# Building the weights' float32 on one core in another way: two bitwise DVE steps with an operand in PSUM, no GpSimd multiplication

## The chip, the cores and the metric

The kernel runs on one core of one Trainium2 chip. The metric is the device time of one execution in microseconds (us); the time of a kernel is the median of several runs. PE is TensorE, DVE is VectorE, ACT is ScalarE, POOL is GpSimd, SP is the engine that issues the DMAs.

## The reference

```python
scores = q @ k.T / 8                                  # 4 batches, 8 heads, 576 rows, 64 per head
scores = where(scores >= max(scores) - tau, scores, -1e9)
x = softmax(scores) @ v                               # (4, 576, 512)
u = x + (relu(x.T @ w_tok1) @ w_tok2).T               # 576 -> 256 -> 576, over the rows
u = u + relu(u @ w_ch1) @ w_ch2                       # 512 -> 1536 -> 512
h = relu(u @ w_in)                                    # 512 -> 1024
out = (h * sigmoid(conv3(h, conv_w))) @ w_out         # 1024 -> 512
```

q, k, v are float32. The six weights arrive as float64, which no engine computes with: a value is two 32-bit words, 8 bytes apart from the next. Each weight is turned on the chip into two float16 matrices, a high part and a low part (the rest), and a product is made of three matmuls: high with high, high with low, low with high.

## The kernel before, in words

The four batches run one after the other, and each has two parts. `attention(b)` (L432) goes through 36 slots of 128 query rows (4 pairs of heads, 9 slots each). For a slot, `scores` (L279) makes matmuls into two PSUM banks, `exps` (L300) takes the maximum on DVE (L303) and the exponential on ACT (L315), `mask` (L319) multiplies with the mask on DVE (L322), `ph` (L324) makes the float16 high part on ACT (L327), `rest` (L329) the low part on POOL (L331) and a transposing DMA, and `pv` (L338) multiplies with v into bank 7. After a pair of heads, `tok` (L379) computes the token mixing, with one bank at a time from the list `free`.

`dense(b)` (L486) has four loops: L526 (u with w_ch1, 24 groups of 12 matmuls), L544 (with w_ch2, 8 groups of 36), L577 (with w_in, 16 groups of 12) and L601 (with w_out). Each group takes a bank from `free` (`dbank`, L271, the oldest first). The evacuation of a group is issued after the next group's matmuls (`flush`, L478), and then the bank goes back into `free`. Evacuations are ACT and then DVE for L526 (L500, L501), DVE for most of L544 (L508 and what follows), ACT for L577 (L553). While `dense(b)` runs, the steps of `attention(b + 1)` are issued between its groups.

Of the 8 PSUM banks, attention 0 uses 0 to 5 for scores in turn (L282), later batches 0 to 3; bank 7 takes `pv`; bank 6 is in `free` from the start. When attention 0 is through with its scores, L459 adds banks 4 and 5:

```python
free = [6]                                # L269
free.extend((4, 5))                       # L459
```

The weights are converted in 47 chunks of at most 512 columns: 3 of w_tok1, 4 of w_tok2 (288 columns each), 12 of w_ch1, 12 of w_ch2, 8 of w_in, 8 of w_out. `wload` (L142) is a generator: its first step issues the DMA into a staging tile `st` (3 buffers), its second all the arithmetic. `wstep` (L166) does one second step and one more first step. It is called eight times in attention 0 (`W0`, L616), once for each of the 12 rounds of L526, three times for each of the 4 rounds of L544, twice for each of the 8 rounds of L577, all in batch 0. A scheduler that works ahead of the run puts the instructions into the engines' queues by a simulated time, so that a chunk can stand earlier in a queue than in the program; each queue is worked off in order.

For a chunk `load_f32` (L107) does: ACT multiplies the high word, read as a float32, by 256 in place (L125); DVE shifts the high word by 3 and masks it (L126); DVE masks the high word and sets an exponent (L128); DVE adds the top three bits of the low word (L134, or for w_tok1 and w_tok2 a DVE shift, L131, and a POOL addition, L132); POOL multiplies the two (L137). Then ACT rounds to float16, the high part (L150), and POOL subtracts it from the float32, the low part (L151). The float32 lies in a tile `wf` with two buffers.

Of the kernel before, what the change touches and what calls it, by code (L numbers as in the profile page):

```python
# [8 lines left out]
F32 = mybir.dt.float32  # L9
F16 = mybir.dt.float16  # L10
I32 = mybir.dt.int32
AF = mybir.ActivationFunctionType
# [6 lines left out]
def kernel(ctx: ExitStack, tc: tile.TileContext, q, k, v, tau,  # L19
# [7 lines left out]
    nc = tc.nc  # L27
# [19 lines left out]
    WS = 2.0 ** UP  # L47
    SX = VSC / ONE
    UDS = 1.0 / (WS * WS)

# [56 lines left out]
    def load_f32(src, o, n, up=0, early=False):  # L107

        if src.dtype == F32:
            g = tmpp.tile([P, 512], F32, tag="wf", name="wf")
            nc.sync.dma_start(g[:, :n], src[:, o:o + n])
            return lambda: g[:, :n]
        st = stage.tile([P, 512, 2], I32, tag="st", name="st")
        with hold("w"):
            nc.sync.dma_start(st[:, :n].rearrange("p n w -> p (n w)"), src.bitcast(I32)[:, 2 * o:2 * (o + n)])

        def bits():
            lo, hi = st[:, :n, 0], st[:, :n, 1]
            f = tmpp.tile([P, 512], I32, tag="wf", name="wf")
            f, hf = f[:, :n], hi.bitcast(F32)
            A.activation(out=hf, in_=hf, func=AF.Copy, scale=256.0)  # L125
            V.tensor_scalar(out=f, in0=hi, scalar1=3, scalar2=0x3FFFFFF8,  # L126
                            op0=ALU.logical_shift_left, op1=ALU.bitwise_and)
            V.tensor_scalar(out=hi, in0=hi, scalar1=-0x40000000, scalar2=(63 + up) << 23,  # L128
                            op0=ALU.bitwise_and, op1=ALU.bitwise_or)
            if early:  # L130
                V.tensor_scalar(out=lo, in0=lo, scalar1=29, scalar2=None, op0=ALU.logical_shift_right)  # L131
                G.tensor_tensor(out=f, in0=f, in1=lo, op=ALU.add)  # L132
            else:
                V.scalar_tensor_tensor(out=f, in0=lo, scalar=29, in1=f,  # L134
                                       op0=ALU.logical_shift_right, op1=ALU.bitwise_or)
            f = f.bitcast(F32)
            G.tensor_tensor(out=f, in0=f, in1=hf, op=ALU.mult)  # L137
            return f

        return bits  # L140

    def wload(src, dst, o, n):  # L142
        wide = src.dtype != F32
        f = load_f32(src, o, n, UP if wide else 0, src in (w_tok1, w_tok2))
        yield
        f = f()
        hi, lo = [d[:, o:o + n] for d in dst]
        if not wide:
            G.tensor_scalar(out=f, in0=f, scalar1=WS, scalar2=1.0, op0=ALU.mult, op1=ALU.mult)
        A.activation(out=hi, in_=f, func=AF.Copy)  # L150
        G.tensor_tensor(out=lo, in0=f, in1=hi, op=ALU.subtract)  # L151
        yield
# [6 lines left out]
    for src, pr, step in ((w_tok1, wt1, 512), (w_tok2, wt2, 288), (w_ch1, wc1, 512),  # L159
                                (w_ch2, wc2, 512), (w_in, wi, 512), (w_out, wo, 512)):  # L160
        tot = src.shape[1]
        wq += [(src, flat(pr), o, min(step, tot - o)) for o in range(0, tot, step)]

    wrun = []

    def wstep(n):  # L166

        for _ in range(n):
            while wq and len(wrun) < 3:
                wrun.append(wload(*wq.pop(0)))  # L170
                next(wrun[-1])
            if wrun:
                next(wrun.pop(0))
            if wq:
                wrun.append(wload(*wq.pop(0)))
                next(wrun[-1])
# [255 lines left out]
    def attention(b):  # L432
# [18 lines left out]
        while i < c1 + LAG or todo:  # L451
# [3 lines left out]
            if c0 <= i - 1 < c1:  # L455
                mask(i - 1)
                ph(i - 1)
                if i == PER:
                    free.extend((4, 5))  # L459
# [232 lines left out]
```

## Time and profile before

| | us |
|---|---|
| median of 3 runs | 836.05 (835.38 to 837.16) |
| the profiled execution | 839.7 |
| its span, first to last instruction | 837.9 |
| busy in the span: PE, DVE, ACT, POOL | 735.2, 598.1, 478.0, 452.8 |

The busy share of an engine over the whole span is a mean over stages with different limits: attention 0 with nothing dense beside it, then four dense parts, the first with the conversion of the weights, the last with no attention beside it. So the views of single stretches say more than the sums. A busy instruction of DVE or POOL can contain waiting for the other.

### The profile page before, as it was taken

What the parts mean: (1) busy time and instruction counts of PE and PEld (TensorE: products, weight loads), DVE (VectorE), ACT (ScalarE), POOL (GpSimd) and SP (SyncE); (2) the same over time, 40 slices, a digit from 0 to 9 for tenths busy, and PEclk for the clock granted to TensorE, in tenths of its full rate; (3) what the DMA queues carried; (4) which work ended last, traced back from release to release, by engine and by line L of the source; (5) the groups of instructions that cost most, each with busy time, mean ns of one, the idle gap of its engine ahead of it and who ended that gap; (6) DMA issues with size and microseconds to landing.
All of it is one profiled execution on the core that took longest, in us unless ns stands there. A gap on an engine that the chain in (4) does not pass through costs nothing. (4 is left out here: it accounts for less than half of the span.)

```text
span 837.9 us, 18667 instructions
## 1 busy us (share of the span) xinstructions
PE 735.2 (88%) x7376; PEld 552.4 (66%) x7376; DVE 598.1 (71%) x954; ACT 478.0 (57%) x993; POOL 452.8 (54%) x444
## 2 busy tenths in 40 slices
PE   4767858788878667999999988999999999999988
PEld 2555646567656555577888765677888765787754
DVE  6898988999999999525777797257775881232370
ACT  6867866565566676534656676346655762220361
POOL 5878887788888889611545465124545640000041
PEclk8998999999999998999999999999999999999999
DMA  6999899888898762423767753326644411000001
GB/s 205 216 181 220 166 204 257 193 215 201 198 197 188 193 145 63 100 64 81 146 137 142 148 109 71 86 51 142 131 82 79 74 31 51 8 1 1 2 1 56
DMA packets 197543, 101.38 MB, mean 121 GB/s; under 512 B 174544, under 2 KB 178128, under 8 KB 197456
## 3 DMA queue, kind: packets, MB, share of 16 engines
q1 hardware_dynamic: 197456, 100.20, 54.8%
q8 instruction: 57, 0.93, 0.5%
q14 instruction: 30, 0.25, 0.1%
HBM read 42.36 MB, written 4.72 MB: 56 GB/s over the span
## 5 line engine op out<-in xcount | busy, mean ns | idle before, releaser
L331 POOL TENSOR_TENSOR ph<-e,ph 128x576 f16<-128x576 f32 x108 | 150.2, 1393 | 110.6 <-ACT ph L327 98.2
L544 PE MATMUL ps<-act_t,wc_h 128*128 128x256 f16 (+1 forms) x768 | 151.7, 288 | 0.0
L526 PE MATMUL ps<-u_h,wc_h 128*128 128x256 f16 (+1 forms) x384 | 110.5, 288 | 11.0 <-DVE act_t L501 10.9
L322 DVE SCALAR_TENSOR_TENSOR e<-ps,thr,e 128x576 f32<-128x576 f32 x108 | 87.2, 811 | 42.7 <-ACT e L315 22.1
L303 DVE TENSOR_REDUCE nm<-ps 128x1 f32<-128x576 f32 x144 | 107.3, 746 | 12.5 <-PE ps L291 10.7
L567 POOL TENSOR_TENSOR act_t<-ct,act_t 128x576 f16<-128x576 f32 x32 | 45.5, 1421 | 125.9 <-ACT act_t L566 122.9
L526 PE MATMUL ps<-u_l,wc_h 128*128 128x256 f16 (+1 forms) x384 | 110.5, 288 | 0.7 <-DVE u_l L411 0.7
L544 PE MATMUL ps<-act_t,wc_l 128*128 128x256 f16 (+1 forms) x384 | 110.5, 288 | 0.0
L526 PE MATMUL ps<-u_h,wc_l 128*128 128x256 f16 (+1 forms) x384 | 110.4, 288 | 0.0
L327 ACT ACTIVATE ph<-e 128x576 f16<-128x576 f32 x108 | 73.3, 680 | 58.1 <-DVE e L322 32.8
L291 PE MATMUL ps<-kt,qt 128*128 128x288 f16 (+1 forms) x480 | 76.2, 296 | 20.4 <-DVE e L322 20.3
L311 POOL TENSOR_SCALAR thr<-nm,mtaus 128x1 f32<-128x1 f32 x108 | 52.0, 482 | 73.0 <-DVE nm L303 67.9
L501 DVE SCALAR_TENSOR_TENSOR act_t<-ps,act_t 128x256 f16<-128x256 f32 (+1 forms) x96 | 43.2, 452 | 64.7 <-ACT act_t L500 64.6
L526 PEld LDWEIGHTS <-wc_h 128*128 128x128 f16 x768 | 75.0, 98 | 21.4 <-issue 2.3
L544 PEld LDWEIGHTS <-wc_h 128*128 128x128 f16 x768 | 75.4, 98 | 19.8 <-issue 0.9
L346 PE MATMUL ps<-vh,pt 128*128 128x65 f16 (+1 forms) x1080 | 73.3, 196 | 12.9 <-DVE x L366 8.0
L315 ACT ACTIVATE e<-ps,bias 128x576 f32<-128x576 f32 x108 | 79.7, 738 | 8.1 <-POOL ph L331 2.1
L577 PE MATMUL ps<-u_h,wi_h 128*128 128x256 f16 (+1 forms) x256 | 75.7, 296 | 9.8 <-ACT h L553 4.6
L562 DVE SCALAR_TENSOR_TENSOR ct<-h,cw,ct 128x576 f32<-128x576 f32 x64 | 77.1, 1205 | 9.5 <-ACT ct L560 8.7
L601 PE MATMUL ps<-wo_h,act_t 128*128 128x512 f16 x256 | 77.3, 381 | 1.2 <-POOL act_t L567 0.7
L577 PE MATMUL ps<-u_h,wi_l 128*128 128x256 f16 (+1 forms) x256 | 75.8, 296 | 0.0
L577 PE MATMUL ps<-u_l,wi_h 128*128 128x256 f16 (+1 forms) x256 | 75.7, 296 | 0.0
(111 smaller groups left out, 1720.8 us busy)
## 6 DMA issues: line engine op xcount, KB each, us to landing
st<-in_moe_w_ch_dram SPq DMA_DIRECT2D x24, 512.0 KB, 4.7
ld<-in_v_dram SPq DMA_DIRECT2D x32, 288.0 KB, 3.9
kt<-ks SPq DMA_DIRECT2D x48, 144.0 KB, 2.7
st<-in_moe_w_in_dram SPq DMA_DIRECT2D x8, 512.0 KB, 4.1
st<-in_moe_w_out_dram SPq DMA_DIRECT2D x8, 512.0 KB, 4.3
out_dram<-ot SPq DMA_DIRECT2D x16, 256.0 KB, 2.0
ld<-in_q_dram SPq DMA_DIRECT2D x12, 288.0 KB, 3.7
ld<-in_k_dram SPq DMA_DIRECT2D x12, 288.0 KB, 3.4
```

The source lines that it names most:

```text
L291: T.matmul(s3[o:o + m, a], st["qt"][:, hh, q0:q0 + m], st["kt"][hh][:, x, a * hn:(a + 1) * hn], start=(x == 0), stop=(x == 1))
L303: crit["max"] = V.tensor_reduce(out=nm, in_=c["s3"], axis=AX.XY, op=ALU.max, negate=True)
L315: crit["exp"] = A.activation(out=e.rearrange("p (a b) -> p a b", a=2), in_=c["s3"], func=AF.Exp, bias=bias, scale=sc)
L322: crit["mask"] = V.scalar_tensor_tensor(out=e3, in0=c["s3"], scalar=c["thr"], in1=e3, op0=ALU.is_ge, op1=ALU.mult)
L327: A.activation(out=c["ph"][:, 0:S], in_=c["e"], func=AF.Copy)
L331: G.tensor_tensor(out=c["ph"][:, S:], in0=c["e"], in1=c["ph"][:, 0:S], op=ALU.subtract)
L346: T.matmul(dst[o:o + m], pt[:, j, o:o + m], vh[:, hh, j, 0:D + 1], start=(j == 0), stop=(j == NSL - 1))
L526: T.matmul(t, wc1[wx][:, f, c], u[c][ux][:, sl], start=(c == 0 and i == 0), stop=(c == NC - 1 and i == 2))
L544: T.matmul(t, wc2[wx][:, c, f], r_t(f, rx)[:, sl], start=(by_dve(c) and f == 0 and i == 0), stop=(f == NF - 1 and i == 2))
L562: V.scalar_tensor_tensor(out=ct, in0=ht[:, kk:kk + S], scalar=cw[:, kk, f:f + 1], in1=ct, op0=ALU.mult, op1=ALU.add)
L577: T.matmul(t, wi[wx][:, f, c], u[c][ux][:, s0:s0 + n], start=(c == 0 and i == 0), stop=(c == NC - 1 and i == 2))
L601: T.matmul(t, g_t(f, gx)[:, j * P:(j + 1) * P], wo[wx][:, f], **lim)
```

## The change

`wload` now starts a chunk in `load_hl`, which gives two views of the staging tile: the upper 16 bits of the low word as unsigned 16-bit integers, and the high word. `float32` then issues four instructions. ACT multiplies the high word, read as a float32, by a power of two in place. ACT takes the top three bits of the low word as an integer, written as 32-bit integers to `f`. DVE shifts the high word by 3 and ors it with `f` into `f`. DVE masks the sign of the high word and ors it with `f` into `w`. For the first 8 chunks that are issued (`W1`) `f` is the tile `wf` in SBUF; for all others it is bank 4 of PSUM (`CB`). The scale of a weight is now 2^4 for w_tok1 and w_ch1, and 2^8 for the others. With 2^8, `w` is `wf` and holds the scaled value: ACT rounds it to the high part and POOL subtracts. With 2^4, `w` is `f` (the bank or `wf`), ACT scales while it rounds, and DVE scales and subtracts. Bank 4 no longer comes into `free` when attention 0 ends but when the last chunk is done, in the last round of L577. conv_w, 24 columns, goes the same way in SBUF.

```diff
--- before.py
+++ after.py
@@ -9,6 +9,7 @@
 F32 = mybir.dt.float32
 F16 = mybir.dt.float16
 I32 = mybir.dt.int32
+U16 = mybir.dt.uint16
 AF = mybir.ActivationFunctionType
 ALU = mybir.AluOpType
 AX = mybir.AxisListType
@@ -45,8 +46,10 @@
     ONE = 0.125
     UP = 4
     WS = 2.0 ** UP
+    UP2 = 8
+    WS2 = 2.0 ** UP2
     SX = VSC / ONE
-    UDS = 1.0 / (WS * WS)
+    UDS = 1.0 / (WS * WS2)
 
     const = ctx.enter_context(tc.tile_pool(name="const", bufs=1))
     wts = ctx.enter_context(tc.tile_pool(name="wts", bufs=1))
@@ -104,79 +107,92 @@
     def hold(x):
         return tc.issue_after(turn[behind[x]].ins) if behind.get(x) in turn else nullcontext()
 
-    def load_f32(src, o, n, up=0, early=False):
-
-
-
-
-
-        if src.dtype == F32:
-            g = tmpp.tile([P, 512], F32, tag="wf", name="wf")
-            nc.sync.dma_start(g[:, :n], src[:, o:o + n])
-            return lambda: g[:, :n]
+    ps = psum.tile([P, 8, 512], F32, name="ps")
+    CB = 4
+
+    def load_hl(src, o, n):
+
         st = stage.tile([P, 512, 2], I32, tag="st", name="st")
         with hold("w"):
             nc.sync.dma_start(st[:, :n].rearrange("p n w -> p (n w)"), src.bitcast(I32)[:, 2 * o:2 * (o + n)])
-
-        def bits():
-            lo, hi = st[:, :n, 0], st[:, :n, 1]
-            f = tmpp.tile([P, 512], I32, tag="wf", name="wf")
-            f, hf = f[:, :n], hi.bitcast(F32)
-            A.activation(out=hf, in_=hf, func=AF.Copy, scale=256.0)
-            V.tensor_scalar(out=f, in0=hi, scalar1=3, scalar2=0x3FFFFFF8,
-                            op0=ALU.logical_shift_left, op1=ALU.bitwise_and)
-            V.tensor_scalar(out=hi, in0=hi, scalar1=-0x40000000, scalar2=(63 + up) << 23,
-                            op0=ALU.bitwise_and, op1=ALU.bitwise_or)
-            if early:
-                V.tensor_scalar(out=lo, in0=lo, scalar1=29, scalar2=None, op0=ALU.logical_shift_right)
-                G.tensor_tensor(out=f, in0=f, in1=lo, op=ALU.add)
-            else:
-                V.scalar_tensor_tensor(out=f, in0=lo, scalar=29, in1=f,
-                                       op0=ALU.logical_shift_right, op1=ALU.bitwise_or)
-            f = f.bitcast(F32)
-            G.tensor_tensor(out=f, in0=f, in1=hf, op=ALU.mult)
-            return f
-
-        return bits
-
-    def wload(src, dst, o, n):
-        wide = src.dtype != F32
-        f = load_f32(src, o, n, UP if wide else 0, src in (w_tok1, w_tok2))
+        halves = st[:, :n].rearrange("p n w -> p (n w)").bitcast(U16).rearrange("p (n w) -> p n w", w=4)
+        return halves[:, :, 1], st[:, :n, 1]
+
+    def wload(src, dst, o, n, up, bank=None):
+
+
+
+
+
+
+        hi, lo = [d[:, o:o + n] for d in dst]
+        w = tmpp.tile([P, 512], F32, tag="wf", name="wf")[:, :n]
+        if src.dtype == F32:
+            nc.sync.dma_start(w, src[:, o:o + n])
+            yield
+            G.tensor_scalar(out=w, in0=w, scalar1=2.0 ** up, scalar2=1.0, op0=ALU.mult, op1=ALU.mult)
+            whole = True
+        else:
+            lw, hw = load_hl(src, o, n)
+            yield
+            whole = up % 8 == 0
+            f = ps[:, bank, :n] if bank is not None else w
+            if not whole:
+                w = f
+            float32(w, f, lw, hw, up // 8)
+        A.activation(out=hi, in_=w, func=AF.Copy, scale=1.0 if whole else 2.0 ** up)
+        if whole:
+            G.tensor_tensor(out=lo, in0=w, in1=hi, op=ALU.subtract)
+        else:
+            V.scalar_tensor_tensor(out=lo, in0=w, scalar=2.0 ** up, in1=hi, op0=ALU.mult, op1=ALU.subtract)
         yield
-        f = f()
-        hi, lo = [d[:, o:o + n] for d in dst]
-        if not wide:
-            G.tensor_scalar(out=f, in0=f, scalar1=WS, scalar2=1.0, op0=ALU.mult, op1=ALU.mult)
-        A.activation(out=hi, in_=f, func=AF.Copy)
-        G.tensor_tensor(out=lo, in0=f, in1=hi, op=ALU.subtract)
-        yield
+
+    def float32(w, f, lw, hw, up8):
+
+        fi, wi32 = f.bitcast(I32), w.bitcast(I32)
+        hf = hw.bitcast(F32)
+        A.activation(out=hf, in_=hf, func=AF.Copy, scale=2.0 ** (up8 - 112))
+        A.activation(out=fi, in_=lw, func=AF.Copy, scale=2.0 ** -13, bias=2.0 ** -14 - 0.5)
+        V.scalar_tensor_tensor(out=fi, in0=hw, scalar=3, in1=fi,
+                               op0=ALU.logical_shift_left, op1=ALU.bitwise_or)
+        V.scalar_tensor_tensor(out=wi32, in0=hw, scalar=-0x80000000, in1=fi,
+                               op0=ALU.bitwise_and, op1=ALU.bitwise_or)
 
     def flat(pr):
         return [t.rearrange("p a b -> p (a b)") if len(t.shape) == 3 else t.rearrange("p a b c -> p (a b c)")
                 for t in pr]
 
     wq = []
-    for src, pr, step in ((w_tok1, wt1, 512), (w_tok2, wt2, 288), (w_ch1, wc1, 512),
-                                (w_ch2, wc2, 512), (w_in, wi, 512), (w_out, wo, 512)):
+    for src, pr, step, up in ((w_tok1, wt1, 512, UP), (w_tok2, wt2, 288, UP2), (w_ch1, wc1, 512, UP),
+                              (w_ch2, wc2, 512, UP2), (w_in, wi, 512, UP2), (w_out, wo, 512, UP2)):
         tot = src.shape[1]
-        wq += [(src, flat(pr), o, min(step, tot - o)) for o in range(0, tot, step)]
-
+        wq += [(src, flat(pr), o, min(step, tot - o), up) for o in range(0, tot, step)]
+    W1 = 8
     wrun = []
+    total = len(wq)
+
+    def wnext():
+        x = wq.pop(0)
+        wrun.append(wload(*x, bank=None if total - len(wq) <= W1 else CB))
+        next(wrun[-1])
 
     def wstep(n):
 
         for _ in range(n):
             while wq and len(wrun) < 3:
-                wrun.append(wload(*wq.pop(0)))
-                next(wrun[-1])
+                wnext()
             if wrun:
                 next(wrun.pop(0))
             if wq:
-                wrun.append(wload(*wq.pop(0)))
-                next(wrun[-1])
+                wnext()
+        if n and not wrun and CB not in free:
+            free.append(CB)
 
     cw = const.tile([P, 3 * NG], F32, name="cw")
-    V.tensor_copy(out=cw, in_=load_f32(conv_w, 0, 3 * NG)())
+    if conv_w.dtype == F32:
+        nc.sync.dma_start(cw, conv_w)
+    else:
+        float32(cw, cw, *load_hl(conv_w, 0, 3 * NG), 0)
     cw = cw.rearrange("p (k g) -> p k g", k=3)
 
 
@@ -456,7 +472,7 @@
                 mask(i - 1)
                 ph(i - 1)
                 if i == PER:
-                    free.extend((4, 5))
+                    free.append(5)
             yield
             if c0 <= i - LAG < c1:
                 pv(i - LAG)
@@ -550,7 +566,7 @@
                             late.append((bk, lambda c=c, sl=sl, t=t: u_out(c, sl, t)))
                         yield
         def h_out(f, s0, n, t):
-            A.activation(out=h_t[f % 2][:, 1 + s0:1 + s0 + n], in_=t, func=AF.Relu, scale=1.0 / WS)
+            A.activation(out=h_t[f % 2][:, 1 + s0:1 + s0 + n], in_=t, func=AF.Relu, scale=1.0 / WS2)
             if s0:
                 gate(f, h_t[f % 2])
 
@@ -583,7 +599,7 @@
         def o_out(j, t):
             ot = p2.tile([P, S], F32, tag="ct", name="ot")
             n = C if j < NS else hc
-            A.activation(out=ot[:, :n], in_=t, func=AF.Copy, scale=0.5 / (SX * WS))
+            A.activation(out=ot[:, :n], in_=t, func=AF.Copy, scale=0.5 / (SX * WS2))
             if j < NS:
                 nc.sync.dma_start(out[b, j * P:(j + 1) * P], ot[:, :n])
             else:
```

## Rows read from the trace of the kernel before

**Rows 1.** One line's instructions, L526 in 134:194 and L577 in 268:336.

```profile
L526 PE MATMUL ps<-u_h,wc_h x96: 269/290/471, 134.1 to 193.8; 128*128 128x256 f16 x48, 128*128 128x320 f16 x48
...
L577 PE MATMUL ps<-u_l,wi_h x64: 271/299/472, 267.8 to 335.4; 128*128 128x256 f16 x32, 128*128 128x320 f16 x32
```

**Rows 2.** Windows: length, busy of PE, PEld, DVE, ACT, POOL; PEclk, DMA share, GB/s.

```profile
0.00:134.00 134.00, 90.91 (x992) 66.77 (x993) 115.37 (x206) 96.08 (x198) 104.75 (x105) 0.92 0.94 202
134.00:336.00 202.00, 157.85 (x1603) 121.53 (x1602) 199.16 (x289) 132.28 (x273) 172.97 (x148) 0.93 0.79 182
363.00:510.00 147.00, 141.65 (x1626) 115.68 (x1624) 106.15 (x177) 90.11 (x193) 67.52 (x78) 1.00 0.57 118
```

**Rows 3.** Windows, instructions on tile st alone: length, busy of DVE, ACT, POOL.

```profile
0.00:134.00 134.00, 35.62 (x46) 9.12 (x16) 22.67 (x22) 0.92 0.94 202
134.00:336.00 202.00, 84.31 (x98) 21.48 (x32) 45.67 (x33) 0.93 0.79 182
```

**Rows 4.** Groups by line, DVE, 134:336: count | busy us, mean ns | idle before, releaser.

```profile
L134 DVE SCALAR_TENSOR_TENSOR wf<-st,wf 128x512 int32<-128x512 int32 x33 | 33.9, 1027 | 0.0
L126 DVE TENSOR_SCALAR wf<-st 128x512 int32<-128x512 int32 x32 | 26.8, 839 | 1.6 <-POOL wc_l L151 1.0 <-POOL wi_l L151 0.4
L128 DVE TENSOR_SCALAR st<-st 128x512 int32<-128x512 int32 x33 | 26.7, 809 | 0.2
...
L562 DVE SCALAR_TENSOR_TENSOR ct<-h,cw,ct 128x576 f32<-128x576 f32 x12 | 14.8, 1229 | 0.0
```

**Rows 5.** DVE in order of time: start us, us, line, op.

```profile
76.89 1.38 DVE L126 TENSOR_SCALAR wf<-st 128x512 int32<-128x512 int32 x1
...
151.50 0.41 DVE L126 TENSOR_SCALAR wf<-st 128x512 int32<-128x512 int32 x1
151.95 0.43 DVE L128 TENSOR_SCALAR st<-st 128x512 int32<-128x512 int32 x1
152.29 0.69 DVE L134 SCALAR_TENSOR_TENSOR wf<-st,wf 128x512 int32<-128x512 int32 x1
...
156.57 0.41 DVE L501 SCALAR_TENSOR_TENSOR act_t<-ps,act_t 128x256 f16<-128x256 f32 x1
...
160.98 0.48 DVE L501 SCALAR_TENSOR_TENSOR act_t<-ps,act_t 128x320 f16<-128x320 f32 x1
```

**Rows 6.** One line's instructions, whole span: duration ns min/median/max, first and last start.

```profile
L322 DVE SCALAR_TENSOR_TENSOR act_t<-ps,thr,act_t x36: 800/804/819, 11.3 to 106.4; 128x576 f32<-128x576 f32 x36
...
L562 DVE SCALAR_TENSOR_TENSOR ct<-h,cw,ct x64: 801/820/1945, 281.7 to 815.9; 128x576 f32<-128x576 f32 x64
```

**Rows 7.** Groups by line, ACT, 134:336.

```profile
L125 ACT ACTIVATE st<-st 128x512 f32<-128x512 f32 x32 | 21.5, 675 | 9.8 <-DMA st<-in_moe_w_ch_dram 7.0 <-DMA st<-in_moe_w_in_dram 2.3 <-DMA st<-in_moe_w_out_dram 0.5
L150 ACT ACTIVATE wc_h<-wf 128x512 f16<-128x512 f32 x17 | 10.6, 626 | 3.3 <-POOL wf L137 3.2
```

**Rows 8.** Groups by line, POOL, 134:336.

```profile
L137 POOL TENSOR_TENSOR wf<-wf,st 128x512 f32<-128x512 f32 x33 | 45.7, 1384 | 19.4 <-issue 12.8 <-DVE wf L134 4.3 <-POOL wf L137 0.7
```

**Rows 9.** PE in order of time, the first matmul of four groups of L526.

```profile
149.91 0.27 PE L526 MATMUL ps<-u_h,wc_h 128*128 128x256 f16 x1 [1.13 <-DVE act_t L501]
...
151.22 0.30 PE L526 MATMUL ps<-u_h,wc_h 128*128 128x320 f16 x1
...
153.43 0.27 PE L526 MATMUL ps<-u_h,wc_h 128*128 128x256 f16 x1
...
157.04 0.30 PE L526 MATMUL ps<-u_h,wc_h 128*128 128x320 f16 x1 [1.35 <-DVE act_t L501]
```

**Rows 10.** Waits, 134:336: who waited for whom, us in total, times, longest.

```profile
ACT bias L308 <- DVE nm L303: 20.7, 18, 4.1
...
PE ps L526 <- DVE act_t L501: 10.5, 9, 2.2
```

**Rows 11.** Groups by line, DVE, 363:510.

```profile
L501 DVE SCALAR_TENSOR_TENSOR act_t<-ps,act_t 128x256 f16<-128x256 f32 (+1 forms) x24 | 10.9, 452 | 15.9 <-ACT act_t L500 15.9
```

## The prediction

> **What bounds the kernel now.** I read the busy time by stretch first, then the DVE's groups in the worst stretch, then its instructions in order of time, then the waits. Batch 0's dense part runs its first two matmul loops and the third (L526 to L577) from 134.1 to 335.4 us [rows 1]. In that stretch of 202 us the DVE is busy for 199.2, POOL for 173.0, PE for 157.9 and ACT for 132.3. Batch 1's same loops, with the same work of attention beside them but no weights to convert, take 147 us, with PE at 141.7 and DVE at 106.2; PE's granted clock is 0.93 in the one stretch and 1.00 in the other [rows 2]. So dense 0 is 55 us longer, and the engine that has no idle time left in it is the DVE. The reader should see next what fills it: instructions on the weights' staging tile take 84.3 us of the DVE there, and 35.6 us ahead of it [rows 3]. By line they are L134, L126 and L128, 33.9 + 26.8 + 26.7 = 87.4 us for 33 chunks, 2.65 us per chunk (the two sums differ by overlapping ends) [rows 4].
>
> The same three instructions are much shorter when POOL happens to be idle beside them: 0.41, 0.43 and 0.69 us in one chunk, against means of 0.84, 0.81 and 1.03 [rows 4, 5]. L322, which has one operand in PSUM, doesn't vary: 0.800 to 0.819 us in all 36 between 11.3 and 106.4 us, while POOL is busy 104.8 of 134 us [rows 2, 6]. So the long DVE instructions are those with all operands in SBUF, and the difference is waiting for POOL, counted as busy.
>
> **The change part by part.** Everything is summed against the profiled execution (839.7 us, span 837.9), which is 3.65 us or 0.4% over the median of 836.05; savings are taken off the median.
>
> *DVE, 134 to 336 us.* Out go the three instructions of 33 chunks: 87.4 us. In come two for each of the 28 chunks of w_ch2, w_in and w_out, three for the 5 of w_ch1 that are left by then (17 L150 of w_ch fall in the stretch [rows 7], 12 of them w_ch2's). Each has 512 columns and an operand in PSUM. No row has a bitwise DVE instruction reading PSUM, and none has a DVE write to PSUM. The nearest rows are L134 unhindered, the same shape at 0.69 us, and L322 with a PSUM operand, 576 columns at 0.80 [rows 5, 6]. I take 0.69, since column count matches. 28 x 2 x 0.69 + 5 x 3 x 0.69 = 49.0 us, at 0.80 it is 56.8. Gain 38 us (31 at the other end; below 31 only if PSUM writes were slow, which no row shows or excludes).
>
> *POOL and what waits for it.* L137 goes: 45.7 us of POOL's 173 [rows 2, 8], and the subtraction of w_ch1. L562 takes 1.229 us in this stretch against 0.801 at its shortest, 12 times: 5.1 us of waiting [rows 4, 6]. If that shrinks with POOL's load (some 30%) it is 1.5 us; the other lines with two SBUF inputs I estimate at as much again and a little more: 4 us together, bounds 0 and 10.
>
> *Rule against the change.* The unhindered L126 and L128 run 512 columns in 0.41 and 0.43 us, L134 in 0.69 [rows 5]. The Trainium skill, "VectorE: DVE Perf Modes", section "Why PSUM operands drop a tier", says that a float32-sized operand in PSUM takes an instruction back to one element per cycle; by that the two fast instructions are given up for slow ones. The trace agrees on the fast pair, 0.41 against 0.69. By unhindered durations alone a chunk goes from 1.53 to 1.38 us, w_ch1's from 1.53 to 2.07, and the sum would be 28 x 0.15 - 5 x 0.54 = 1.5 us. I take the measured means instead, since the DVE's queue pays them.
>
> *ACT.* One more instruction per chunk: 33 x 0.65 us (between L150's 0.626 and L125's 0.675 [rows 7]) = 21.5, so 132.3 becomes 153.8 us. Between 0 and all of it can show; beside a DVE at 157 I cost it at nothing, and the cover is thin: 3 us. The writing to bank 4 also adds a wait: the next chunk's ACT write stands until the DVE (for w_ch1 also ACT's copy and the third DVE step) is through with the bank, and exp, relu and bias of attention and dense are queued behind it on ACT. For w_ch1 the third DVE step waits for ACT's copy, with the masks and maxima behind it.
>
> *The bank that is missing.* Dense 0 turns over banks 6 and 5 where it had 6, 4 and 5, until the last chunk is done. A group of L526 then must wait for the evacuation of the group before the last. In the trace the groups that start at 149.91 and 151.22 are evacuated by L501 at 156.98 and 161.46, while the groups two later start at 153.43 and 157.04 [rows 5, 9]: with two banks they would have started 3.6 and 4.4 us later. With three banks PE waits for L501 10.5 us in all [rows 10]. In batch 1 the DVE is the one that waits, 15.9 us for ACT, so L501 is never late there [rows 11]. So the price is between 0 and 4 us for each of 24 groups, 0 to 96. It comes from the queue that stands in front of the evacuation on the DVE; with the DVE at nine tenths and not full I take 0.5 us, nearer to batch 1: 12 us. L544's groups of 36 matmuls hide an evacuation, and L577's are evacuated by ACT alone; both are left at nothing, covered by PE's own group, else they add to the range's upper end.
>
> *Ahead of 134 us.* 35.6 us of the DVE's 115.4 (of 134) are conversions [rows 2, 3]. The seven small chunks have no bank: their two or three DVE steps have all operands in SBUF and keep waiting for POOL, but POOL loses an addition and a multiplication each. Later w_ch1 chunks, now started from 76.89 us on [rows 5], must wait until attention 0 leaves bank 4; its last mask starts at 106.4 [rows 6]. That lightens attention 0 and loads the time behind it. DMA issues on SP keep their number and order; a stage tile held longer delays the next load, hidden by three buffers. I take 4 us (0 to 10).
>
> Sum: the stretch goes 202 - 38 - 4 + 12 = 172 us (DVE 157 busy, ACT 154, PE at least 142 to 147), and 4 ahead of it: 34 us, 836.05 - 34 = **802 us**.
>
> **Rivals.**
> B, full release: the shorter DVE queue makes the evacuations punctual, as in batch 1. For it: L501 there is never late. Against: three engines at nine tenths. 836 - 46 = 790.
> C, ACT becomes the bound: 154 us of work, and of its 70 us idle now 20.7 are one wait for the maxima [rows 10], a chain that stays. Keeping 33 of the 70 (the 20.7 and a third of the rest, an estimate) puts the stretch at 154 + 33 = 187: gain 15 + 4, 817.
> D, it doesn't do what it says: the DVE's waits for POOL only move to other instructions with two SBUF inputs, since POOL's L331 and subtractions remain. Then the unhindered durations count, 1.5 us: 834.5. Against: L137 itself leaves, and L322 shows what an operand in PSUM does. The Trainium skill's rule above ("VectorE: DVE Perf Modes") would give the same time.
> E, slower: the missing bank. PE starts a group only when the DVE has emptied the one before the last, and attention's scores stand behind that group on PE, so maxima and masks come late and the DVE idles. It decides from 46/24 = 1.9 us per group; at 2.3, over half of the 3.6 and 4.4 seen, it costs 55: 836 - 46 + 55 = 845.
>
> **How the numbers follow.** My forecast has 0.52, B 0.15, C 0.14, D 0.06, E 0.13. The forecast's own range is 794 to 812 (banks at 0.2 to 0.9 us per group; the 0.80 us end of the DVE steps alone gives 809). The range 786 to 828 takes in B and C with their bounds and leaves out D and E, 0.19. A measurement of this kernel can tell about 0.2% (1.7 us) from no change. Faster by more than that: forecast, B, C and a third of D, 0.83; within it, the rest of D, 0.04; slower, E, 0.13.
>
> **What the changed profile would show.** Right: two DVE instructions of about 0.69 us per chunk with a narrow spread, no POOL multiplication; DVE under 95% between the first L526 and the last L577 of batch 0; that stretch near 172 us; PE's waits for L501's counterpart at 10 to 25 us. Wrong: the new DVE instructions above 0.8 us or spread like L134's (D); ACT without idle time (C); PE waiting 40 us or more for evacuations while the DVE has gaps (E).

## The result and the profile after

The changed kernel takes 824.03 us, the median of four runs (819.77 to 825.58), against 836.61 us for the kernel before beside them: a ratio of 0.984 (95% interval 0.980 to 0.988), or 12.6 us less. The forecast was 802 us, 34 us less. The sign is right, the time lies in the range, and about two thirds of the gain isn't there.

The profiled execution took 823.18 us (span 821.4, against 837.9 before). Where the 16.5 us of the spans lie: dense 0's first matmul starts at 124.1 us instead of 134.1, so 10 us come from the time ahead of it; dense 1 starts at 356.4 instead of 363.0, so 3 of these 10 are lost again within dense 0, the loop with w_out included; 10 more come after it, where 56 of attention's masks are left instead of 65. The windows of the profile after (length, busy of PE, PEld, DVE, ACT, POOL, then PEclk, DMA share, GB/s) answer to [rows 2]; dense 0's first three loops now run from 124.1 to 331.9:

```profile
0.00:124.00 124.00, 89.72 (x1006) 66.06 (x1007) 105.73 (x191) 97.47 (x208) 68.06 (x74) 0.94 0.98 209
124.00:332.00 208.00, 170.04 (x1789) 128.00 (x1786) 179.03 (x297) 165.28 (x344) 123.44 (x131) 0.96 0.88 205
...
257.00:356.00 99.00, 80.06 (x761) 54.16 (x761) 79.99 (x116) 76.14 (x155) 66.55 (x64) 0.91 0.71 162
```

The forecast stretch of 172 us is one of 208. Yet the DVE is no longer full: 179 of 208 us is 86%, where it was 199 of 202. POOL fell from 173 to 123 us. The stretch also holds more of attention's work than before (41 masks on the DVE, the counterpart of L322, against 33).

The DVE's groups in that stretch (line, op, tiles, count | busy us, mean ns | idle before and who ended it), answering to [rows 4]:

```profile
L156 DVE SCALAR_TENSOR_TENSOR ps<-st,ps 128x512 int32<-128x512 int32 x36 | 24.8, 689 | 10.3 <-ACT ps L155 10.0
L158 DVE SCALAR_TENSOR_TENSOR wf<-st,ps 128x512 int32<-128x512 int32 x28 | 19.0, 680 | 0.6
L578 DVE SCALAR_TENSOR_TENSOR ct<-h,cw,ct 128x576 f32<-128x576 f32 x14 | 14.8, 1054 | 0.9 <-ACT ct L576 0.8
...
L158 DVE SCALAR_TENSOR_TENSOR ps<-st,ps 128x512 int32<-128x512 int32 x8 | 5.5, 688 | 0.1
L147 DVE SCALAR_TENSOR_TENSOR wc_l<-ps,wc_h 128x512 f16<-128x512 f32 x8 | 5.4, 679 | 0.2 <-ACT wc_h L143 0.2
```

And the instructions on the staging tile over the whole span (duration ns min/median/max, first and last start):

```profile
L155 ACT ACTIVATE ps<-st x39: 602/621/656, 102.3 to 320.9; 128x512 int32<-128x512 uint16 x39
L156 DVE SCALAR_TENSOR_TENSOR ps<-st,ps x39: 677/687/705, 103.3 to 324.2; 128x512 int32<-128x512 int32 x39
L158 DVE SCALAR_TENSOR_TENSOR wf<-st,ps x28: 670/678/693, 192.0 to 327.9; 128x512 int32<-128x512 int32 x28
```

Each of the two steps takes what was forecast (0.69 us, here 0.670 to 0.705) and hardly varies, while POOL is busy 59% of the time. The Trainium skill, "SBUF — State Buffer", section "Who interferes with whom", says that a DVE instruction with two inputs in SBUF contends with GpSimd instructions that read SBUF, and that one with at most one SBUF input does not, outside the modes in which it takes both ports. The trace agrees: with both inputs in SBUF the same step has a mean of 999 ns (first experiment).

So the DVE got its relief, and the time did not follow. The first thing to suspect is when bank 4 becomes free: L155 writes it from 102.3 us on and not before.

### The profile page after: what moved, and what is told of

Read it like the earlier page. It is cut to its first block, busy times and chain, and to the rows that moved or that the text cites. A ratio compares the mean times of both kernels' runs of the same rounds, so it can differ in the third digit from the quotient of the medians.

```text
span 821.4 us, 18594 instructions
## 1 busy us (share of the span) xinstructions
PE 733.6 (89%) x7376; PEld 549.1 (67%) x7376; DVE 549.3 (67%) x920; ACT 496.1 (60%) x1041; POOL 346.3 (42%) x374
## 5 line engine op out<-in xcount | busy, mean ns | idle before, releaser
L347 POOL TENSOR_TENSOR ph<-e,ph 128x576 f16<-128x576 f32 x108 | 145.1, 1348 | 137.2 <-ACT ph L343 120.7
L560 PE MATMUL ps<-act_t,wc_h 128*128 128x256 f16 (+1 forms) x768 | 149.7, 288 | 3.0 <-ACT u_h L426 2.7
L542 PE MATMUL ps<-u_h,wc_h 128*128 128x320 f16 (+1 forms) x384 | 109.7, 286 | 3.4 <-DVE act_t L517 2.3
L542 PE MATMUL ps<-u_h,wc_l 128*128 128x320 f16 (+1 forms) x384 | 109.7, 286 | 0.8 <-DVE wc_l L147 0.8
L560 PE MATMUL ps<-act_t,wc_l 128*128 128x320 f16 (+1 forms) x384 | 110.3, 288 | 0.0
L542 PE MATMUL ps<-u_l,wc_h 128*128 128x320 f16 (+1 forms) x384 | 109.7, 286 | 0.0
L307 PE MATMUL ps<-kt,qt 128*128 128x288 f16 (+1 forms) x480 | 72.8, 287 | 10.6 <-DVE e L338 10.2
L578 DVE SCALAR_TENSOR_TENSOR ct<-h,cw,ct 128x576 f32<-128x576 f32 x64 | 73.3, 1146 | 8.8 <-ACT ct L576 8.0
L327 POOL TENSOR_SCALAR thr<-nm,mtaus 128x1 f32<-128x1 f32 x108 | 39.0, 361 | 95.1 <-DVE nm L319 85.9
L362 PEld LDWEIGHTS <-pt 128*128 128x128 f16 (+1 forms) x1080 | 62.9, 101 | 21.4 <-DMA pt<-ph 12.6
```

Source lines behind the costliest of these rows:

```text
L307: T.matmul(s3[o:o + m, a], st["qt"][:, hh, q0:q0 + m], st["kt"][hh][:, x, a * hn:(a + 1) * hn], start=(x == 0), stop=(x == 1))
L347: G.tensor_tensor(out=c["ph"][:, S:], in0=c["e"], in1=c["ph"][:, 0:S], op=ALU.subtract)
L362: T.matmul(dst[o:o + m], pt[:, j, o:o + m], vh[:, hh, j, 0:D + 1], start=(j == 0), stop=(j == NSL - 1))
L542: T.matmul(t, wc1[wx][:, f, c], u[c][ux][:, sl], start=(c == 0 and i == 0), stop=(c == NC - 1 and i == 2))
L560: T.matmul(t, wc2[wx][:, c, f], r_t(f, rx)[:, sl], start=(by_dve(c) and f == 0 and i == 0), stop=(f == NF - 1 and i == 2))
L578: V.scalar_tensor_tensor(out=ct, in0=ht[:, kk:kk + S], scalar=cw[:, kk, f:f + 1], in1=ct, op0=ALU.mult, op1=ALU.add)
```

## The experiments

All times are medians, all ratios against the kernel before on the same chip (its medians were 837 to 839 us).

| kernel | us | ratio (95%) |
|---|---|---|
| e1: all float32 in SBUF, banks 6, 4, 5 for dense 0 | 813.2 | 0.971 (0.968 to 0.975) |
| e2: all float32 in SBUF, banks 6, 5 | 812.0 | 0.969 (0.964 to 0.974) |
| e3: before, with banks 6, 5 | 841.5 | 1.006 (1.004 to 1.008) |
| e4: bank 4 for chunks from w_ch2 on | 811.1 | 0.969 (0.965 to 0.973) |
| e5: after, bank 4 not back before the w_out loop | 820.7 | 0.980 (0.977 to 0.984) |
| e6: e4 and e5 | 811.9 | 0.970 (0.967 to 0.973) |
| e7: one SBUF tile in place of bank 4 | 832.7 | 0.995 (0.992 to 0.997) |
| e8: e1 and an unread POOL multiplication per chunk | 835.5 | 0.998 (0.996 to 1.000) |
| e9: e5, every other chunk in SBUF | 810.0 | 0.967 (0.965 to 0.968) |
| e10: e6, every other chunk in SBUF | 816.7 | 0.974 (0.972 to 0.976) |
| e11: before without POOL's multiplication | 815.3 | 0.972 (0.971 to 0.974) |
| e12: e2 with three SBUF tiles | 819.1 | 0.977 (0.975 to 0.979) |
| e13: e5, w_ch1's chunks in SBUF | 811.1 | 0.968 (0.965 to 0.971) |
| e14: e5, bank 4 held for two DVE steps, not three | 821.2 | 0.981 (0.977 to 0.984) |
| e15: e2 with one constant moved (control of e7, e8, e12) | 815.9 | 0.973 (0.970 to 0.976) |

**Is it the bank or the new arithmetic?** e1 keeps the arithmetic and gives the bank back to the matmuls, e2 keeps the arithmetic alone, e3 takes the bank alone.

```diff
 e1, e2
-        wrun.append(wload(*x, bank=None if total - len(wq) <= W1 else CB))
+        wrun.append(wload(*x, bank=None))
 e1 also
-                    free.append(5)
+                    free.extend((4, 5))
-        if n and not wrun and CB not in free:
-            free.append(CB)
 e3, in the kernel before
-                    free.extend((4, 5))
+                    free.append(5)
...
+        if n and not wrun and 4 not in free:
+            free.append(4)
```

> The changed kernel with the float32 of every chunk in SBUF and banks 6, 4, 5 for dense 0, as before the change. Theory BANK (the missing third bank ate the gain: a w_ch1 group of dense 0 starts only when the group before the last is evacuated): the 24 w_ch1 groups of dense 0, 66 us in the changed kernel, take 58 us or less, although the DVE's steps are stretched by POOL again (mean about 1.0 us instead of 0.69); in all 815 to 828 us. Theory CHAIN (the conversion's own chain over ACT and one bank paces dense 0, the third bank is worth nothing): the w_ch1 groups stay at 62 us or more, in all 826 to 836 us.

> As the run with SBUF and three banks, but bank 4 lies idle until the last chunk is done, so that dense 0 has two banks. Nothing else differs. BANK: 8 to 20 us slower than with three banks, most of it in the w_ch1 groups of dense 0. CHAIN: within 3 us of it. Against the changed kernel it shows what the operand in PSUM alone is worth: by the DVE's durations 40 x 2 x 0.3 = 24 us of DVE time.

> The kernel before, with bank 4 idle until the last chunk is done: the missing bank by itself, under the old conversion. BANK: 8 to 25 us slower than before (845 to 861 us), the w_ch1 groups of dense 0 at 68 us or more instead of 60. CHAIN: within 3 us of before.

Without PSUM as scratch the new arithmetic gains 24 us, twice what the change gained. A third bank for dense 0 makes no difference under it (e1 and e2 overlap) and 0.6%, about 5 us, under the old one (e3). So a missing bank is not where the gain went; sending the chunks through bank 4 is what costs. (e1 came out faster than both of its stated ranges, and e3 between its two.) The length of a single loop would have misled here: e1's w_ch1 loop takes 53.8 us and e2's 66.0, as a missing bank would have it, but the one holds 8 of attention's masks and the other 14, and in the w_ch2 loop it is 76.8 with 15 against 57.8 with 9. The DVE's groups of e1, 124 to 311 us, show the steps that are slower there and still beat the change:

```profile
L156 DVE SCALAR_TENSOR_TENSOR wf<-st,wf 128x512 int32<-128x512 int32 x34 | 34.0, 999 | 3.8 <-ACT wf L155 3.7
L158 DVE SCALAR_TENSOR_TENSOR wf<-st,wf 128x512 int32<-128x512 int32 x34 | 32.8, 965 | 0.2
...
L576 DVE SCALAR_TENSOR_TENSOR ct<-h,cw,ct 128x576 f32<-128x576 f32 x12 | 12.8, 1064 | 0.0
```

**Which chunks does the bank hurt?** e4 leaves w_ch1 in SBUF and takes bank 4 out of the matmuls' list only when the w_ch2 loop begins; e5 hands it back only ahead of the w_out loop, so that the last w_in group isn't put into the bank that the last chunk still needs; e6 does both. (`W1` of 20 takes in the seven small chunks, the 12 of w_ch1 and one of w_ch2.)

```diff
 e4
-    W1 = 8
+    W1 = 20
-                    free.append(5)
+                    free.extend((4, 5))
...
+        if b == 0:
+            flush()
+            free.remove(CB)
 e5
-        if n and not wrun and CB not in free:
-            free.append(CB)
...
+        if b == 0:
+            free.append(CB)
+
         def o_out(j, t):
```

> The changed kernel, but the first 20 chunks (up to the last that is converted in the w_ch1 groups) have their float32 in SBUF, dense 0 has three banks for its w_ch1 groups, and bank 4 is taken away only for the groups after that. BANK: the w_ch1 groups take 50 to 58 us, in all 810 to 818 us, faster than the changed kernel's 824. CHAIN: no faster than the changed kernel, 822 to 830 us, since the DVE steps of 12 chunks of w_ch1 wait for POOL again.

> The changed kernel, with bank 4 given back to dense 0 after the last w_in group instead of in the round before. Theory HANDBACK (the last w_in group gets bank 4 and waits there for the last w_out chunk, 317 to 328.7 us in the changed kernel, and with it the last gate, the output groups and dense 1): the last w_in group follows the one before it, dense 1 starts 6 to 12 us earlier, in all 812 to 818 us. Theory ONE TILE (all later chunks pass through one bank, one after the other, so the conversions end at 328 us instead of about 280): nothing changes, 821 to 827 us.

> The kernel with bank 4 taken away only after the w_ch1 groups, and in addition given back after the last w_in group. HANDBACK: its last two w_in groups stood until 311 us for the last chunk, so 2 to 6 us faster than that kernel's 811, 804 to 809 us. ONE TILE: 809 to 813 us, as without it.

e4 and e6 are as fast as e1 and e2: from w_ch2 on, one bank for all chunks costs nothing. e5 stays near the changed kernel. The stall that it removes is real, one wait of 3.4 us in the changed kernel (PE's timeline: start, us, line, [idle before <- who ended it]):

```profile
328.67 0.42 PE L593 MATMUL ps<-u_h,wi_h 128*128 128x320 f16 x1 [3.41 <-DVE wf L158]
```

but the ratios of the change and of e5 have overlapping intervals, so what it is worth isn't shown.

**PSUM, or one place for all chunks?** e7 puts the float32 that went to bank 4 into a single SBUF tile, which is free from the start; a 128x128 constant (`idf`) shares a `wf` buffer for want of room. e8 asks about POOL: e1 with a multiplication per chunk that nobody reads.

```diff
 e7
-            f = ps[:, bank, :n] if bank is not None else w
+            f = (tmpp.tile([P, 512], F32, tag="f1", name="f1", bufs=1)[:, :n] if bank is not None else w)
 e8 (e1 and)
+        G.tensor_tensor(out=scr[:, :n], in0=w, in1=w, op=ALU.mult)
...
+    scr = const.tile([P, 512], F32, name="scr")
 e7, e8, e12, e15
-    idf = const.tile([P, P], F32, name="idf")
+    idf = tmpp.tile([P, 512], F32, tag="wf", name="idf")[:, :P]
```

> The changed kernel, with one tile of SBUF of the same size in the place of bank 4 for the chunks' integers (dense 0 has two banks as there; bank 4 lies idle until the last chunk is issued). ONE TILE: as slow as the changed kernel or slower, 820 to 830 us, with the conversions ending after 310 us. HANDBACK: near the run with two SBUF tiles and two banks (812 us), 809 to 816 us, since no bank has to be waited for.

> The run with SBUF and three banks (813 us), with one POOL multiplication of the chunk added whose result nobody reads: POOL has its load of before again, the DVE keeps two or three steps per chunk. If the gain of the SBUF kernels comes from POOL's multiplication being gone (DVE steps with all operands in SBUF wait for POOL): 825 to 836 us. If it comes from one DVE step less per chunk: 813 to 820 us.

e7's single tile is worse than the bank: 832.7 us against 815.9 for the same code with two buffers (e15), 17 us for the second place alone, and more than either theory expected of it. So it isn't PSUM that is slow. e8 loses 0.0266 of 837 us against e1, 22 us, for an instruction with no reader; the moved constant may be some 4 us of it (e15 against e2), which leaves 18. POOL and DVE in e8 (129 to 329 and 124 to 330 us, groups by line):

```profile
L144 POOL TENSOR_TENSOR scr<-wf 128x512 f32<-128x512 f32 x34 | 38.1, 1121 | 12.1 <-DVE wf L159 11.3 <-DVE rc L378 0.7
```

```profile
L159 DVE SCALAR_TENSOR_TENSOR wf<-st,wf 128x512 int32<-128x512 int32 x35 | 40.3, 1151 | 0.2
L157 DVE SCALAR_TENSOR_TENSOR wf<-st,wf 128x512 int32<-128x512 int32 x35 | 36.5, 1044 | 3.9 <-ACT wf L156 3.8
...
L578 DVE SCALAR_TENSOR_TENSOR ct<-h,cw,ct 128x576 f32<-128x576 f32 x12 | 17.2, 1432 | 0.0
```

Against e1 the two steps went from 999 and 965 to 1044 and 1151 ns, and the convolution's step, which has nothing to do with weights, from 1064 to 1432. Against the kernel before, e8 has a DVE step less for most chunks and a POOL multiplication as well, and takes 0.998 of its time: with the multiplication there, the DVE step shows 2 us (the moved constant may hide some 4 more).

**How much of it is POOL's multiplication, and do two places help?** e11 is the kernel before without that one instruction (its weights then lack their scale and sign). e9 and e10 put every other later chunk into SBUF; e12 gives e2 a third tile.

```diff
 e11, in the kernel before
-            G.tensor_tensor(out=f, in0=f, in1=hf, op=ALU.mult)
 e9 (e5 and), e10 (e6 and)
-        wrun.append(wload(*x, bank=None if total - len(wq) <= W1 else CB))
+        wrun.append(wload(*x, bank=None if total - len(wq) <= W1 or len(wq) % 2 else CB))
 e12 (e2, the moved constant, and)
-    tmpp = ctx.enter_context(tc.tile_pool(name="tmpp", bufs=2))
+    tmpp = ctx.enter_context(tc.tile_pool(name="tmpp", bufs=3))
```

> The changed kernel with bank 4 given back after the last w_in group, and with every other later chunk in SBUF instead of bank 4, so that two chunks can be under way. Theory ONE TILE (a single place for all later chunks paces the conversions; that, not the DVE's durations, sets when dense 0 ends): the last chunk is done before 305 us instead of 324, in all 806 to 814 us, against 821 with bank 4 alone. Theory BANK COST (what an operand in PSUM costs is tied to the bank, to dense 0's two banks or the writes to PSUM): 816 to 824 us.

> The kernel that takes bank 4 only from the w_ch2 groups on and gives it back after the last w_in group (812 us), with every other later chunk in SBUF. ONE TILE: the last chunk done before 300 us instead of 313, in all 803 to 810 us. BANK COST: 810 to 814 us, as without it.

> The kernel before without POOL's multiplication (its weights then lack their scale and sign); the three DVE steps and all else stay. If POOL's multiplication is what the conversion costs dense 0: 808 to 820 us, most of what the SBUF kernels gain, without one DVE step less. If the number of DVE steps matters: 826 to 836 us.

> The changed kernel with all chunks' float32 in SBUF and bank 4 idle (812 us with two tiles, 833 with the integers in one), with three tiles. ONE TILE: the step from one to two was most of it, 806 to 813 us. If two were still scarce it falls below 804.

e11 gains 23.6 us on the same chip with all three old DVE steps still in place; no version of the new arithmetic beats it by more than 0.6%. All three steps became shorter: the means of L134, L128 and L126, 1027, 809 and 839 ns in [rows 4], read 880, 707 and 632 in e11's groups from 130 to 313 us, which is 15 us for 33 chunks:

```profile
L134 DVE SCALAR_TENSOR_TENSOR wf<-st,wf 128x512 int32<-128x512 int32 x33 | 29.0, 880 | 0.0
...
L128 DVE TENSOR_SCALAR st<-st 128x512 int32<-128x512 int32 x33 | 23.3, 707 | 0.1
L126 DVE TENSOR_SCALAR wf<-st 128x512 int32<-128x512 int32 x33 | 20.8, 632 | 1.7 <-ACT st L125 1.5
```

e11 also takes a link out of each chunk's chain; e8 adds none, though its tile is held until POOL has read it. So neither is the multiplication quite alone; together they put it at 18 to 24 us.

e9 has the lowest median, 810.0 us, and beats both kernels: 3.3% below the kernel before and 1.8 points of the ratio below the change; by its interval it isn't apart from e2, e4, e6 or e13. e10 and e12 missed. More places were expected to help or do nothing; e10 came out 0.35 points of the ratio behind e6 and e12 0.45 behind e15, with intervals that overlap in both cases.

**Is it w_ch1's chunks in the one place, and for how long they hold it?** e13 is e5 with w_ch1 in SBUF and still two banks for dense 0. e14 is e5 with the second DVE step of w_ch1 writing to SBUF, so that ACT's copy and the third step no longer hold the bank. e15 is the control.

```diff
 e13 (e5 and)
-    W1 = 8
+    W1 = 20
 e14 (e5 and)
-            if not whole:
-                w = f
```

> The changed kernel with bank 4 given back after the last w_in group (821 us) and with the 12 chunks of w_ch1 in SBUF; dense 0 keeps two banks from its start. Theory FIRST CHUNKS (w_ch1's chunks hold bank 4 one at a time through three DVE steps and a copy, so the 20th chunk is done at 193 us and not at 155 to 165, and dense 0 ends late by what is never caught up): the 20th chunk before 172 us, dense 1 from 334 to 341 us, in all 809 to 816 us. Theory THIRD BANK (what helped in the kernel that takes bank 4 only from w_ch2 on was dense 0's third bank): 818 to 824 us, dense 1 from 345 us on.

> The changed kernel with bank 4 given back after the last w_in group (821 us), but the second DVE step of a w_ch1 chunk writes its float32 to SBUF, as for all other weights, so that bank 4 is free again after it; the copy and the third DVE step read SBUF. FIRST CHUNKS: the 20th chunk before 183 us instead of 193, in all 811 to 817 us. If it is not how long the bank is held: 818 to 824 us.

> Control: the kernel with SBUF, two tiles and two banks (812 us), with one edit that does no work after the start: a 128x128 identity of the prologue lies in a float32 tile of the conversion, as in the kernels with one and with three SBUF tiles. What it differs by from 812 us is what another order of the instruction queues alone does to the time; 808 to 818 us expected. If it is 818 or more, the 819 us with three tiles say nothing on the number of tiles; if it is below 815, three tiles are slower than two.

e13 against e5 is one number in the code and 0.980 against 0.968, 10 us, with intervals that don't touch; it also shows again that the third bank doesn't matter (e13 has two, e6 three, 811.1 and 811.9). e14 gains nothing, so how long a chunk holds the bank is not it. Nor is it simply how late the chunks are done. The third step of w_ch1 and the high part of w_out, in e5 and then in e14:

```profile
L147 DVE SCALAR_TENSOR_TENSOR wc_l<-ps,wc_h x11: 673/681/692, 109.3 to 186.9; 128x512 f16<-128x512 f32 x11
L143 ACT ACTIVATE wo_h<-wf x8: 612/624/630, 284.0 to 325.5; 128x512 f16<-128x512 f32 x8
```

```profile
L145 DVE SCALAR_TENSOR_TENSOR wc_l<-wf,wc_h x12: 676/684/1409, 52.8 to 173.9; 128x512 f16<-128x512 f32 x12
L141 ACT ACTIVATE wo_h<-wf x8: 613/628/657, 271.7 to 307.6; 128x512 f16<-128x512 f32 x8
```

e14 is through with w_ch1 13 us earlier and with w_out 18, and takes the same time.

e15 stands 4 us above e2 with intervals that overlap, for a move that removes no work: another order in the queues may be worth that much by itself, and I read no cause into smaller differences, nor a sure one into those of e10 and e12.

The trace shows what e13 does with its freedom, here against the changed kernel, from which it differs by e5's later hand-back too. ACT's high part (L143), one line's instructions over the whole span, in the changed kernel:

```profile
L143 ACT ACTIVATE wc_h<-ps x11: 577/592/648, 106.3 to 185.5; 128x512 f16<-128x512 f32 x11
L143 ACT ACTIVATE wi_h<-wf x8: 612/614/620, 244.9 to 279.3; 128x512 f16<-128x512 f32 x8
L143 ACT ACTIVATE wo_h<-wf x8: 616/626/635, 286.0 to 328.7; 128x512 f16<-128x512 f32 x8
```

and in e13:

```profile
L143 ACT ACTIVATE wc_h<-wf x24: 612/620/632, 51.2 to 216.5; 128x512 f16<-128x512 f32 x24
L143 ACT ACTIVATE wi_h<-wf x8: 612/614/631, 221.0 to 247.4; 128x512 f16<-128x512 f32 x8
L143 ACT ACTIVATE wo_h<-wf x8: 615/628/645, 251.8 to 291.4; 128x512 f16<-128x512 f32 x8
```

The order of chunks is fixed, so the 11 chunks of w_ch1 that must wait for attention 0 to leave bank 4 push all later ones: w_in's begin 24 us later, w_out's last comes 37 us later, at 328.7 against 291.4. In the changed kernel the last of w_ch1 come just in time (ACT, then PE, in order of time):

```profile
177.05 0.58 ACT L143 ACTIVATE wc_h<-ps 128x512 f16<-128x512 f32 x1
...
185.54 0.58 ACT L143 ACTIVATE wc_h<-ps 128x512 f16<-128x512 f32 x1
```

```profile
178.98 0.27 PE L542 MATMUL ps<-u_h,wc_h 128*128 128x256 f16 x1
...
186.17 0.42 PE L542 MATMUL ps<-u_h,wc_h 128*128 128x256 f16 x2 [0.64 <-ACT wc_h L143]
```

where e13 has the last one at 155.64:

```profile
150.41 0.61 ACT L143 ACTIVATE wc_h<-wf 128x512 f16<-128x512 f32 x1
...
155.64 0.63 ACT L143 ACTIVATE wc_h<-wf 128x512 f16<-128x512 f32 x1 [0.49 <-DVE wf L158]
```

The first two loops nevertheless take the same time in both. The difference is behind them: from the start of the w_in loop (257 us in both) to dense 1 it is 99 us in the changed kernel, whose window stands above (PE's clock 0.91, ACT 76 us, DVE 80 us), and 76 us in e13, where conversion has mostly been done by then:

```profile
257.00:333.00 76.00, 67.92 (x655) 46.56 (x654) 61.13 (x89) 58.14 (x120) 52.26 (x49) 0.98 0.67 144
```

In e5, the control with the same hand-back, the like stretch is 90 us, so up to 9 of these 23 us may be the hand-back's:

```profile
257.00:347.00 90.00, 74.34 (x687) 50.19 (x685) 72.69 (x105) 69.64 (x143) 62.55 (x57) 0.92 0.68 157
```

Of the 23 us, 11 are left at the end (spans 821.4 and 810.8): e13 has 63 of attention's masks left when dense 1 starts, the changed kernel 56.

One rival stands untested. The mean granted clock of PE is 0.964 to 0.971 in e5's four runs and 0.979 to 0.983 in e13's. In their profiled executions (spans 815.2 and 810.8) PE is busy 736.4 and 730.0 us with the same number of matmuls, and idle 78.8 and 80.8 us, so there the difference is time of matmuls and not gaps. Whether w_ch1's way through the bank lowers the clock, or the clock differs for another reason, no run separates.

## Why the prediction was wrong, by its steps

**DVE, 134 to 336 us (38 us): the durations held, the worth didn't.** The new steps cost 24.8 + 19.0 + 5.5 + 5.4 = 54.7 us for 36 chunks, 1.52 each where 49.0/33 = 1.48 was forecast, and 0.69 rather than 0.80 was the right row. But the 38 us were put on the path one for one, because the DVE was busy 199 of 202 us. e11 has the three old steps, e2 and e15 the two new ones in SBUF, e6 and e13 mostly the narrow ones in PSUM: 815, 812 and 816, 812 and 811 us. With POOL's multiplication gone, fewer and shorter conversion steps are worth 0 to 5 us (e9 is the fastest), and with it there, e8 shows 2. This is the step that failed first: a busy time that is part waiting was counted as work, and the removal of work as the gain.

**POOL and what waits for it (4 us, bounds 0 to 10): 18 to 24 us.** This was the largest term and it was taken for a side effect. e11 (-23.6) and e8 (+22 without a reader, perhaps 4 of it the moved constant) measure it from both sides. The text had the observation in hand, that the DVE's long steps are waiting for POOL, and then sized the relief by one line, L562, and put the other lines that meet POOL at about as much by an estimate without a row. That line did come down as it said, 1.229 to 1.054 us, 12 to 14 times, 2 us. What it left at nothing is the queue of POOL itself. Which share belongs to the DVE's waits and which to POOL's own queue (attention's low parts stand in it) the runs don't separate.

**The bank that is missing (+12 us): about nothing.** e1 against e2 and e6 against e13 show no cost for it under the new arithmetic; under the old, 5 us (e3). In the changed kernel's waits from 124 to 332 us, PE waits 2.1 us for the evacuation's counterpart, not the 10 to 25 us forecast:

```profile
PE ps L593 <- DVE wf L158: 3.4, 1, 3.4
...
PE ps L542 <- DVE act_t L517: 2.1, 5, 0.5
```

**Ahead of 134 us (4 us), and the wait for bank 4 (nothing): -10 us there, 10 to 13 us lost behind.** Here is the second failure. "That lightens attention 0 and loads the time behind it" got no price for the load behind; the wait was costed as ACT standing behind the DVE for the bank, and no such wait is among ACT's from 100 to 332 us. Nor did the 10 us ahead come from the later start: e1 and e13 don't wait for bank 4 with w_ch1, and their dense 0 starts at 124.3 and 125.1 us. A stage tile held longer was left at nothing, rightly: ACT's waits for the staging loads rose from 16.6 to 28.3 us over the span, but they are 25.3 and 26.5 in e4 and e13, which are fast. What costs is w_ch1's way through the one place: 10 us by e13 against e5, 17 by e7 against e15, where all chunks after the first 8 go through a single SBUF tile. How it costs stays open. Argued, and not shown, is the lost lead: in a fixed order, chunks that had started at 77 us start at 102, and all later ones are pushed. For one chunk at a time speaks e7, which starts early and is worse; against both, that bank 4 alone from w_ch2 on costs nothing, and that e14, with a shorter hold and earlier ends, gains nothing. The granted clock, above, may hold part of it.

Sum by what was measured: -18 to -24 for the multiplication, 0 to -5 for the DVE's steps, 0 for the bank count, +10 for w_ch1 through one place: -8 to -19; measured -12.6. That 824 lies within 786 to 828 is luck. Errors partly cancel: 33 to 38 us too much for the DVE, 14 to 20 too little for POOL, 12 for a bank that cost nothing, and a loss of 10 that had no price.

**Rivals.** B (790) needed the DVE's relief to be worth its length. C (817) named ACT; ACT has 43 us to spare in the 208, the faster e13 has the same ACT instruction, and e11 lacks it (ACT 133.7 of 183 us) and is no faster than e13, so C's neighbouring time is a coincidence. D is refuted by the spread of 670 to 705 ns, though it was right that the DVE's busy time is not what the kernel pays. E's mechanism, the missing bank, is there and small.

What sets the 811 us that five versions share stays open. The DVE is busy 95% of the like stretch in e1 and 98% in e11 (179.3 of 183), and e13, where it is 87% (163.8 of 188), is no faster than e1 beyond the intervals, so it isn't simply the DVE.

## What to carry to other kernels

When an engine's busy time contains waiting for another engine, price the removal of the other engine's instruction by an experiment or by all the lines that meet it, not by one; it can be worth more than the instructions that are being rewritten: here 18 to 24 us against 0 to 5. When a change routes a pipeline of producers through one scratch place, write down when that place becomes free and how far ahead of their use the producers ran before, and give it a price; here 11 chunks of w_ch1 and one of w_ch2 cost 10 us, although their DVE steps became shorter. Where a place in two buffers is to be had for those that run ahead, the bank does no harm for the others (e4, e6, e13).

## What the runs showed that I had not expected

A POOL multiplication of 128x512 with no reader, 1.12 us each and 47 chunks of at most that size, cost 18 to 22 us of 836, with a DVE line elsewhere going from 1064 to 1432 ns. Bitwise DVE steps reading or writing PSUM as 32-bit integers are as quick as the same operation unhindered in SBUF (0.69 us for 512 columns), and stay within 0.670 to 0.705 us beside a busy POOL. And moving a constant into another buffer (e15) or adding a third one as well (e12) left the medians 4 and 7 us above e2: in a kernel whose queues a scheduler orders ahead of the run, that is the grain below which a single variant says little. The 10 us of e13 against e5 lie above it, the 0 to 5 us of the DVE's steps within it.
